# Row-block order for two w_out chunks of batch 0, paired P groups, and split output tiles in a one-core attention and MoE kernel

## Chip, cores, metric

One NeuronCore of a Trainium2 chip (trn2). The metric is device time in microseconds (us), the median of several runs of the whole kernel. A profile of one execution also gives a span, about 1.8 us shorter than the time of the same execution (215.9 and 217.67 for the kernel before); it is used for places and differences. In the lines of the profile, PE stands for TensorE's matmuls and PEld for its weight loads, DVE for VectorE, ACT for ScalarE, POOL for GpSimd and SP for SyncE; a q behind a name (SPq) marks the engine's queue of instructions. PSUM is the memory that matmuls write to. L476 is line 476 of that kernel's program.

## The reference

Eight batches, eight heads, 512 tokens and 32 state rows of width 64. Cross attention runs both ways between the tokens and the state; the result, 4352 rows of 512, goes through a feed-forward layer with exact Gelu.

```python
scores = scale * np.matmul(x, state.transpose(0, 1, 3, 2))
a = softmax(scores);  xread = np.matmul(a, state)
a2 = softmax(scale * np.matmul(state, x.transpose(0, 1, 3, 2)))
sread = np.matmul(a2, x)
attn = np.concatenate([xread, sread], axis=2)      # then to rows of H * D = 512
h = attn_rows @ w_in                               # 512 -> 2048
out = (0.5 * h * (1.0 + erf(h * inv_sqrt2))) @ w_out   # 2048 -> 512, float32
```

## The kernel before

The kernel folds w_in into the state: P = state @ w_in per batch, so that h = a @ P. A w_out chunk is four of the sixteen row blocks of h of a batch; a chunk of P is one P group, 512 of its 2048 columns. The order of instructions is written by hand. The pieces that matter:

```python
ps_f = ctx.enter_context(tc.tile_pool(name="ps_f", bufs=4, space=PSUM))   # hp, p_ps, transposes, sread
ps_o = ctx.enter_context(tc.tile_pool(name="ps_o", bufs=4, space=PSUM))   # output tiles, P chunks 3 and 4 of a run

def p_mm(b, f, pool, tag):            # a P group: 8 matmuls of 64x32 tiles, two PSUM buffers
    ps = [pool.tile([128, 512], FP32, name="p_ps", tag=tag) for t in range(2)]
    ...
def p_copy(b, f, ps):
    dst = Ps[b][:, :, f * 512:(f + 1) * 512]
    nc.scalar.copy(out=dst[:, 0, :], in_=ps[0])
    nc.vector.tensor_copy(out=dst[:, 1, :], in_=ps[1])

def mm1(b, m):                        # row block m of h, then Gelu on ScalarE
    hp = ps_f.tile([128, S], FP32, name="hp", tag="f")
    ...                               # two matmuls, P x AT
    nc.scalar.activation(out=gs[b][:, m, :], in_=hp, func=AF.Gelu)

def mm2(b, q, j):                     # output tile j: four row blocks of chunk q, one after the other
    ...
    for m in range(4 * q, 4 * q + 4):
        nc.tensor.matmul(ps, lhsT=gs[b][:, m, j * 128:(j + 1) * 128], rhs=w_out_bf[:, m, :],
                         start=(m == 0), stop=(m == MC - 1))
    if q == 3:
        evac(ps, [(out_rows(b, j), slice(0, 128))])   # VectorE copy, then a DMA from SyncE

# the order for batch 0 (cut); M = mm1 of these blocks, U = mm2
M(0, 1, 2, 3); U(0, 1, 2); pmat(0, 1); U(3)
...
M(10, 11); U(8); pmat(0, 3); U(9); atr(1); U(10); M(12, 13); srt(1); M(14, 15); U(11); pmat(1, 0)
...
U(12); state_prep(2, B); M(16); pmat(1, 1); U(13); M(17); U(14); M(18, 19); U(15)
burst([(1, 2), (1, 3), (2, 0), (2, 1)])
# steady pattern for batches 1 to 7 (cut)
mm2_sr(0); mm2_sr(1); U(*range(16 * B - 4, 16 * B - 1)); mm2_last(B - 1, SJ - 1)   # the last DMA leaves from ScalarE's queue
```

The softmax here doesn't subtract the row's maximum and nothing guards it: scores larger than these inputs give would overflow.

Of the kernel before, what the change touches and what calls it, by code (L numbers as in the profile page):

```python
# [9 lines left out]
FP32 = mybir.dt.float32  # L10
# [7 lines left out]
def kernel(  # L18
# [8 lines left out]
    nc = tc.nc  # L27

    B, H, S, D = x.shape
    _, _, NS, _ = state.shape  # L30
    d_model, d_ff = moe_w_in.shape
# [3 lines left out]
    MC = d_ff // 128  # L35
    SJ = S // 128
# [9 lines left out]
    ps_o = ctx.enter_context(tc.tile_pool(name="ps_o", bufs=4, space=PSUM))  # L46
# [6 lines left out]
    w_out_bf = persist.tile([128, MC, d_model], BF16, name="w_out_bf")  # L53
# [18 lines left out]
    for c in range(3):  # L72
# [5 lines left out]
        out=xbs[0].rearrange("p (t c) f -> p t c f", t=2)[:, :, 3, :], in_=x0_rows[:, :, 3, :]  # L78
# [56 lines left out]
    def state_prep(b0, b1):  # L135
        if b0 == 0:
            nc.scalar.copy(out=st_bf[:, 0, :, :], in_=st_f)
        n = b1 - b0
        ps = ps_f.tile([128, n, HC, NS], BF16, name="st_ps", tag="f")
        for b in range(b0, b1):  # L140
            nc.tensor.transpose(
                ps[:, b - b0, :, :].rearrange("p c n -> p (c n)"),
                st_bf[:, b, :, :].rearrange("q t d -> q (t d)"),
                ident,
            )
        for t in range(2):
            nc.vector.tensor_copy(
                out=sbd[64 * t:64 * t + 64, b0:b1, :, 32 * t:32 * t + 32].rearrange(
                    "d b c n -> d (b c) n"
                ),  # L150
                in_=ps[64 * t:64 * t + 64, :, :, :].rearrange("d b c n -> d (b c) n"),
            )
# [7 lines left out]
    def begin(b):  # L160
        A = Att()
        atts[b] = A
        A.x4 = x4s[b % 2]
        A.xo = xos[b % 2]
        A.xT = att.tile([128, SJ, HC, 128], BF16, name="xT", tag="xT")
        A.e = att.tile([128, SJ * 2, HC * NS], BF16, name="e", tag="e")
        A.a = att.tile([128, SJ * 2, HC * NS], BF16, name="a", tag="a")
# [133 lines left out]
    def atr(b):  # L301
        A = atts[b]
        A.AT = att.tile([128, SJ, 2, 128], BF16, name="AT", tag="AT")
        for t in range(2):
            ps = ps_f.tile([128, SJ, 128], BF16, name="aT_ps", tag="f")
            for j in range(SJ):
                nc.tensor.transpose(ps[:, j, :], A.a[:, 2 * j + t, :], ident)
            if b == 0 and t == 1:
                nc.scalar.copy(out=A.AT[:, :, t, :], in_=ps)
            else:  # L310
                nc.vector.tensor_copy(out=A.AT[:, :, t, :], in_=ps)
# [9 lines left out]
    def sread(b):  # L321
        A = atts[b]
        pool, tag = (ps_o, "op") if b == B - 1 else (ps_f, "f")
        A.sr = pool.tile([128, 2, 65], FP32, name="sr", tag=tag)
        for t in range(2):
            for j in range(SJ):
                for c in range(HC):
                    nc.tensor.matmul(  # L328
                        A.sr[32 * c:32 * c + 32, t, :],
                        lhsT=A.e[:, 2 * j + t, 32 * c:32 * c + 32],  # L330
                        rhs=A.xo[:, j, c, 1 + 65 * t:66 + 65 * t],
                        start=(j == 0),
                        stop=(j == SJ - 1),
                    )

    def sread_out(b):
        A = atts[b]
        A.srm = att.tile([128, 2, D], BF16, name="srm", tag="srm")
        flat = A.sr.rearrange("q t d -> q (t d)")
        inv = att.tile([128, 2], FP32, name="inv", tag="inv")  # L340
        nc.vector.reciprocal(out=inv, in_=flat[:, 0:130:129])
        nc.vector.tensor_tensor(
            out=A.srm,
            in0=flat[:, 1:129].rearrange("q (t d) -> q t d", t=2),
            in1=inv[:, :].to_broadcast((128, 2, D)),
            op=ALU.mult,
        )
# [11 lines left out]
    def p_mm(b, f, pool, tag):  # L359
        if b not in Ps:  # L360
            Ps[b] = att.tile([128, 2, d_ff], BF16, name="P", tag="P")
        ps = [pool.tile([128, 512], FP32, name="p_ps", tag=tag) for t in range(2)]
        for c in range(HC):
            for t in range(2):
                nc.tensor.matmul(  # L365
                    ps[t][32 * c:32 * c + 32, :],
                    lhsT=sbd[64 * t:64 * t + 64, b, c, 32 * t:32 * t + 32],
                    rhs=w_in_bf[64 * t:64 * t + 64, c, f * 512:(f + 1) * 512],
                    start=True,
                    stop=True,  # L370
                )
        return ps
# [6 lines that stand above are left out]
    def pmat(b, f):  # L379
        p_copy(b, f, p_mm(b, f, ps_f, "f"))  # L380
# [4 lines left out]
    def burst(chunks, b_read=None):  # L385
        done = []
        first = len(chunks) < 4 and b_read is not None
        if first:
            sread(b_read)
        for i, (b, f) in enumerate(chunks):  # L390
            pool, tag = (ps_f, "f") if i < 2 else (ps_o, "op")
            done.append((b, f, p_mm(b, f, pool, tag)))
        for x in done[:2]:
            p_copy(*x)
        if b_read is not None and not first:
            sread(b_read)
        for x in done[2:3]:
            p_copy(*x)
        if b_read is not None:
            sread_out(b_read)  # L400
        for x in done[3:]:
            p_copy(*x)
# [17 lines left out]
    gs = {}  # L420

    def mm1(b, m):
        if m == 0:
            gs[b] = gpool.tile([128, MC, S], BF16, name="g", tag="g")
        hp = ps_f.tile([128, S], FP32, name="hp", tag="f")
        for t in range(2):
            nc.tensor.matmul(  # L427
                hp,
                lhsT=Ps[b][:, t, m * 128:(m + 1) * 128],
                rhs=atts[b].AT[:, :, t, :],  # L430
                start=(t == 0),
                stop=(t == 1),
            )
        nc.scalar.activation(out=gs[b][:, m, :], in_=hp, func=AF.Gelu)  # L434

    ops = {}

    def evac(ps, rows):
        osb = opool.tile([128, d_model], FP32, name="osb", tag="osb")
        nc.vector.tensor_copy(out=osb, in_=ps)  # L440
        for r, src in rows:
            nc.sync.dma_start(out=r, in_=osb[src, :])

    def out_rows(b, j):
        return out[b * SB:b * SB + S, :].rearrange("(p j) n -> j p n", j=SJ)[j]
# [23 lines left out]
    def mm2(b, q, j):  # L469
        if b == B - 1 and j == SJ - 1:  # L470
            return
        if q == 0:
            ops[b, j] = ps_o.tile([128, d_model], FP32, name="op", tag="op")
        ps = ops[b, j]
        for m in range(4 * q, 4 * q + 4):
            nc.tensor.matmul(  # L476
                ps,
                lhsT=gs[b][:, m, j * 128:(j + 1) * 128],
                rhs=w_out_bf[:, m, :],
                start=(m == 0),  # L480
                stop=(m == MC - 1),
            )
        if q == 3:
            evac(ps, [(out_rows(b, j), slice(0, 128))])

    def mm1_sr(m):
        hp = ps_f.tile([128, B * NS], FP32, name="hps", tag="f")
# [10 lines left out]
    def mm2_sr(s):  # L498
        ps = ps_f.tile([128, d_model], FP32, name="ops", tag="f")
        for m in range(MC):  # L500
            nc.tensor.matmul(  # L501
                ps,
                lhsT=g_sr[:, m, s * 128:(s + 1) * 128],
                rhs=w_out_bf[:, m, :],
                start=(m == 0),
                stop=(m == MC - 1),
            )
        rows = []
        for i in range(4):
            r0 = (4 * s + i) * SB + S  # L510
            rows.append((out[r0:r0 + NS, :], slice(32 * i, 32 * i + 32)))
        evac(ps, rows)


    def M(*ms):
        for m in ms:
            mm1(m // MC, m % MC)

    def U(*us):
        for u in us:  # L520
            mm2(u // 16, u % 16 // 4, u % 4)
# [35 lines left out]


    M(0, 1, 2, 3)
    U(0, 1, 2)  # L560
    pmat(0, 1)
    U(3)
    M(4, 5)
    state_prep(1, 2)
    M(6)
# [17 lines left out]
    sread(1)  # L583
    sread_out(1)
    M(10, 11)
    U(8)
    pmat(0, 3)
    U(9)
    atr(1)
    U(10)  # L590
    M(12, 13)
    srt(1)
    M(14, 15)
    U(11)
    pmat(1, 0)
    begin(2)
    rearr(2)
    xtr_dma(2)
    rearr_ones(2)
    U(12)  # L600
    state_prep(2, B)
    M(16)
    pmat(1, 1)
    U(13)
    M(17)
    U(14)
    M(18, 19)
    U(15)
    burst([(1, 2), (1, 3), (2, 0), (2, 1)])


    u = 16
# [72 lines left out]
```

## Time and profile before

| | before |
|---|---|
| time, median (runs beside the changed kernel) | 217.70 us (217.56 to 217.81, 4 runs) |
| span of the profiled execution | 215.9 us |
| TensorE busy | 208.2 us, 96% |
| PE stretch | 197.60 us |
| last landing to end of span | 1.36 us |

The prediction had three of the four runs, with a median of 217.63.

### The profile page before, as it was taken

The numbers are of one execution on the slowest core, as the hardware profiler recorded it, in microseconds if no ns is written. First come the engines' busy times: TensorE is split into PE (matmuls) and PEld (weight loads), VectorE is DVE, ScalarE is ACT, GpSimd is POOL, SyncE is SP. The second block draws the span as 40 slices with busy tenths as digits, with TensorE's granted clock in tenths as the row PEclk, the third lists the DMA queues.
The fourth block names the chain that finished last, engine by engine and source line by source line (L and its number), as shares of the span: only waits on it lengthen the run. The fifth ranks groups of instructions, "written<-read, shape, count | busy, mean of one in ns | idle before, by whom it ended". The sixth has DMA issues, their size and how long they took to land.

```text
span 215.9 us, 3969 instructions
## 1 busy us (share of the span) xinstructions
PE 208.2 (96%) x1638; PEld 103.4 (48%) x1663; DVE 80.4 (37%) x165; ACT 122.7 (57%) x217; POOL 43.5 (20%) x57
## 2 busy tenths in 40 slices
PE   8889999999999999999999999999999999999993
PEld 8535444444444445444444444444444444765442
DVE  4815665724039202840177006900392025000151
ACT  3754846687686447844974477546864444754000
POOL 7583105901123013301321130300000000000000
PEclk9999999999999999999999999999999999999999
DMA  7999999972722591429350963170225013000044
GB/s 186 187 192 206 206 191 135 257 135 52 97 97 100 99 144 43 154 48 153 46 194 3 155 88 145 52 146 0 100 99 52 0 67 130 3 0 0 14 129 151
DMA packets 38723, 22.98 MB, mean 106 GB/s; under 512 B 21936, under 2 KB 34480, under 8 KB 38704
## 3 DMA queue, kind: packets, MB, share of 16 engines
q0 software_dynamic: 13664, 8.23, 27.1%
q1 hardware_dynamic: 24352, 14.09, 24.8%
q10 hardware_dynamic: 688, 0.39, 0.6%
q8 instruction: 13, 0.21, 0.4%
q14 instruction: 6, 0.05, 0.1%
HBM read 17.30 MB, written 8.91 MB: 121 GB/s over the span
## 4 chain that ended last, share of the span: by engine, by line
PE 93%; ACT 3%; DVE 1%; issue 1%
PE op L476 48%; PE hp L427 25%; PE p_ps L365 4%; PE hps L489 3%; PE ops L501 3%; PE warm_ps L132 2%; ACT g L434 2%; PE opl L454 2%; PE pt L271 2%; PE sr L328 1%; PE xT_ps L211 1%; ACT L434 1%; ACT P L376 1%; PE pc L230 0%; DVE xT L216 0%
## 5 line engine op out<-in xcount | busy, mean ns | idle before, releaser
L476 PE MATMUL op<-w_out_bf,g 128*128 128x512 bf16 x471 | 115.5, 379 | 1.7 <-ACT g L434 0.3
L434 ACT ACTIVATE g<-hp 128x512 bf16<-128x512 f32 x128 | 68.8, 602 | 55.3 <-PE hp L427 55.1
L476 PEld LDWEIGHTS <-g 128*128 128x128 bf16 x496 | 47.9, 98 | 58.3 <-ACT g L434 1.9
L427 PE MATMUL hp<-AT,P 128*128 128x512 bf16 x256 | 65.8, 379 | 0.8 <-ACT P L376 0.5
L440 DVE COPY osb<-op 128x512 f32<-128x512 f32 x31 | 21.4, 691 | 83.1 <-PE op L476 83.1
L427 PEld LDWEIGHTS <-P 128*128 128x128 bf16 x256 | 23.5, 98 | 27.4 <-issue 2.0
L377 DVE CAST P<-p_ps 128x512 bf16<-128x512 f32 x31 | 20.0, 683 | 9.4 <-PE p_ps L365 9.3
L376 ACT CAST P<-p_ps 128x512 bf16<-128x512 f32 x31 | 16.3, 595 | 12.0 <-PE p_ps L365 12.0
L175 POOL COPY x<-xb 128x1024 bf16<-128x1024 bf16 x12 | 12.2, 1043 | 31.5 <-DMA xb<-in_x_dram 26.5
L186 POOL COPY xo<-xb 128x1024 bf16<-128x1024 bf16 x12 | 12.2, 1048 | 22.3 <-PE sr L328 22.3
L291 DVE TENSOR_REDUCE cs<-e 128x16 f32<-128x512 bf16 x14 | 9.5, 677 | 3.9 <-ACT e L278 3.9
L365 PE MATMUL p_ps<-w_in_bf,sbd 64*32 64x512 bf16 x248 | 10.3, 382 | 0.0
L278 ACT ACT_TABLE_LOAD x7 | 9.0, 1283 | 2.1 <-issue 1.3
L294 DVE TENSOR_TENSOR a<-e,ics 128x512 bf16<-128x512 bf16 x14 | 9.7, 692 | 0.5
L440 DVE COPY osb<-ops 128x512 f32<-128x512 f32 x2 | 1.4, 692 | 22.5 <-PE ops L501 22.5
L434 ACT ACT_TABLE_LOAD x7 | 9.0, 1283 | 0.1
L465 ACT COPY osb<-opl 128x128 f32<-128x128 f32 x1 | 0.3, 266 | 15.2 <-PE opl L454 15.2
L278 ACT ACTIVATE e<-pt 128x512 bf16<-128x512 f32 x14 | 7.6, 594 | 0.1
L489 PE MATMUL hps<-XSR,w_in_bf 128*128 128x256 bf16 x64 | 7.6, 273 | 0.0
L132 PE MATMUL warm_ps<-warm 128*128 128x128 bf16 x59 | 6.5, 280 | 1.0 <-DVE warm L75 1.0
L501 PE MATMUL ops<-w_out_bf,g_sr 128*128 128x512 bf16 x32 | 7.1, 379 | 0.0
L365 PEld LDWEIGHTS <-sbd 64*32 64x32 bf16 x248 | 3.5, 89 | 7.5 <-issue 6.4
(66 smaller groups left out, 105.2 us busy)
## 6 DMA issues: line engine op xcount, KB each, us to landing
out_dram<-osb SPq DMA_DIRECT2D x31, 256.0 KB, 2.3
xb<-in_x_dram POOLq DMA_DIRECT2D x7, 512.0 KB, 6.0
w_in_bf<-in_moe_w_in_dram POOLq DMA_DIRECT2D x8, 256.0 KB, 9.6
w_out_bf<-in_moe_w_out_dram POOLq DMA_DIRECT2D x4, 512.0 KB, 11.5
x0f<-in_x_dram SPq DMA_DIRECT2D x2, 256.0 KB, 3.3
out_dram<-osb SPq DMA_DIRECT2D x8, 64.0 KB, 1.7
x0f<-in_x_dram ACTq DMA_DIRECT2D x1, 256.0 KB, 4.1
st_bf<-in_state_dram POOLq DMA_DIRECT2D x1, 192.0 KB, 14.3
```

What stands on the lines that cost most here:

```text
L175: nc.gpsimd.tensor_copy(out=A.x4[:, :, :, 64 * t:64 * t + 64].rearrange("p j c d -> p c j d"), in_=src[:, t],)
L186: eng.tensor_copy(out=A.xo[:, :, c0:, 2 + 64 * t:66 + 64 * t].rearrange("p j c d -> p c j d"), in_=src[:, t, c0:],)
L278: nc.scalar.activation(out=A.e[:, :, 64 * half:64 * half + 64], in_=pt.rearrange("p j t c n -> p (j t) (c n)"), func=AF.Exp, scale=scale,)
L365: nc.tensor.matmul(ps[t][32 * c:32 * c + 32, :], lhsT=sbd[64 * t:64 * t + 64, b, c, 32 * t:32 * t + 32], rhs=w_in_bf[64 * t:64 * t + 64, c ...
L376: nc.scalar.copy(out=dst[:, 0, :], in_=ps[0])
L377: nc.vector.tensor_copy(out=dst[:, 1, :], in_=ps[1])
L427: nc.tensor.matmul(hp, lhsT=Ps[b][:, t, m * 128:(m + 1) * 128], rhs=atts[b].AT[:, :, t, :], start=(t == 0), stop=(t == 1),)
L434: nc.scalar.activation(out=gs[b][:, m, :], in_=hp, func=AF.Gelu)
L440: nc.vector.tensor_copy(out=osb, in_=ps)
L476: nc.tensor.matmul(ps, lhsT=gs[b][:, m, j * 128:(j + 1) * 128], rhs=w_out_bf[:, m, :], start=(m == 0), stop=(m == MC - 1),)
L489: nc.tensor.matmul(hp, lhsT=w_in_bf[:, c, m * 128:(m + 1) * 128], rhs=XSR[:, c, :], start=(c == 0), stop=(c == HC - 1),)
L501: nc.tensor.matmul(ps, lhsT=g_sr[:, m, s * 128:(s + 1) * 128], rhs=w_out_bf[:, m, :], start=(m == 0), stop=(m == MC - 1),)
```

## The change

Its intent: the Gelu results of the first and third chunk come more slowly than TensorE uses them, so each ready row block is applied to all four output tiles before the next one is needed; P groups, each of which costs a change of the array's tiling, are gathered; and the last output tile of a batch leaves in two halves.

```diff
--- before.py
+++ after.py
@@ -438,8 +438,8 @@
     def evac(ps, rows):
         osb = opool.tile([128, d_model], FP32, name="osb", tag="osb")
         nc.vector.tensor_copy(out=osb, in_=ps)
-        for r, src in rows:
-            nc.sync.dma_start(out=r, in_=osb[src, :])
+        for r, src, n0, n1 in rows:
+            nc.sync.dma_start(out=r, in_=osb[src, n0:n1])
 
     def out_rows(b, j):
         return out[b * SB:b * SB + S, :].rearrange("(p j) n -> j p n", j=SJ)[j]
@@ -481,7 +481,9 @@
                 stop=(m == MC - 1),
             )
         if q == 3:
-            evac(ps, [(out_rows(b, j), slice(0, 128))])
+            rows = out_rows(b, j)
+            h = d_model // 2 if j == SJ - 1 else d_model
+            evac(ps, [(rows[:, n:n + h], slice(0, 128), n, n + h) for n in range(0, d_model, h)])
 
     def mm1_sr(m):
         hp = ps_f.tile([128, B * NS], FP32, name="hps", tag="f")
@@ -508,8 +510,21 @@
         rows = []
         for i in range(4):
             r0 = (4 * s + i) * SB + S
-            rows.append((out[r0:r0 + NS, :], slice(32 * i, 32 * i + 32)))
+            rows.append((out[r0:r0 + NS, :], slice(32 * i, 32 * i + 32), 0, d_model))
         evac(ps, rows)
+
+
+    def mm2_m(b, m):
+        for j in range(SJ):
+            if m == 0:
+                ops[b, j] = ps_o.tile([128, d_model], FP32, name="op", tag="op")
+            nc.tensor.matmul(
+                ops[b, j],
+                lhsT=gs[b][:, m, j * 128:(j + 1) * 128],
+                rhs=w_out_bf[:, m, :],
+                start=(m == 0),
+                stop=(m == MC - 1),
+            )
 
 
     def M(*ms):
@@ -557,9 +572,10 @@
 
 
     M(0, 1, 2, 3)
-    U(0, 1, 2)
+    for m in range(3):
+        mm2_m(0, m)
     pmat(0, 1)
-    U(3)
+    mm2_m(0, 3)
     M(4, 5)
     state_prep(1, 2)
     M(6)
@@ -583,30 +599,28 @@
     sread(1)
     sread_out(1)
     M(10, 11)
-    U(8)
-    pmat(0, 3)
-    U(9)
+    mm2_m(0, 8)
+    mm2_m(0, 9)
+    burst([(0, 3), (1, 0)])
+    mm2_m(0, 10)
     atr(1)
-    U(10)
     M(12, 13)
     srt(1)
     M(14, 15)
-    U(11)
-    pmat(1, 0)
+    mm2_m(0, 11)
     begin(2)
     rearr(2)
     xtr_dma(2)
     rearr_ones(2)
     U(12)
+    burst([(1, 1), (1, 2)])
+    U(13)
     state_prep(2, B)
-    M(16)
-    pmat(1, 1)
-    U(13)
-    M(17)
+    M(16, 17)
     U(14)
     M(18, 19)
     U(15)
-    burst([(1, 2), (1, 3), (2, 0), (2, 1)])
+    burst([(1, 3), (2, 0), (2, 1)])
 
 
     u = 16
```

## The prediction

> **What bounds the kernel now.** I read the page first, then the chain that ended last, then the waits of the matmul engine, then the instruction timelines of weight loads and ScalarE in the first 45 us, because the change edits nothing later except the last output tile of each batch.
>
> From the page, parts 1, 2 and 4:
>
> ```profile
> PE 208.2 (96%) x1638; PEld 103.4 (48%) x1663; DVE 80.4 (37%) x165; ACT 122.7 (57%) x217; POOL 43.5 (20%) x57
> PE   8889999999999999999999999999999999999993
> PEclk9999999999999999999999999999999999999999
> PE 93%; ACT 3%; DVE 1%; issue 1%
> ```
>
> TensorE is busy for 96% of a 215.9 us span at full granted clock, and 93% of the chain is PE. Only slices 1 to 3 and the last show holes. Each batch after the first runs the same pattern of matmuls back to back, so a reordering can gain only where PE waits. The list of PE's waits names little, but it sees only the matmul rows; a matmul that stands behind a late weight load appears under PEld. So the timeline of weight loads shows more. Columns: start us, length us, engine, line, operation, count, and in brackets the idle time and its releaser. First chunk of w_out, batch 0:
>
> ```profile
> 13.26 0.10 PEld L476 LDWEIGHTS <-g 128*128 128x128 bf16 x1
> 13.51 0.10 PEld L476 LDWEIGHTS <-g 128*128 128x128 bf16 x1 [0.16 <-ACT g L434]
> 14.00 0.10 PEld L476 LDWEIGHTS <-g 128*128 128x128 bf16 x1 [0.39 <-ACT g L434]
> 14.49 1.63 PEld L476 LDWEIGHTS <-g 128*128 128x128 bf16 x9 [0.40 <-ACT g L434]
> ```
>
> and the third chunk:
>
> ```profile
> 27.62 0.10 PEld L476 LDWEIGHTS <-g 128*128 128x128 bf16 x1
> 27.89 0.10 PEld L476 LDWEIGHTS <-g 128*128 128x128 bf16 x1 [0.17 <-ACT g L434]
> 28.38 0.10 PEld L476 LDWEIGHTS <-g 128*128 128x128 bf16 x1 [0.39 <-ACT g L434]
> 28.87 0.10 PEld L476 LDWEIGHTS <-g 128*128 128x128 bf16 x1 [0.40 <-ACT g L434]
> 29.19 0.11 PEld L365 LDWEIGHTS <-sbd 64*32 64x32 bf16 x8 [0.23 <-issue]
> ```
>
> In both, the first output tile walks through four row blocks of g, and each of blocks 1 to 3 is waited for. ScalarE supplies them thus:
>
> ```profile
> 12.38 2.07 ACT L434 ACTIVATE g<-hp 128x512 bf16<-128x512 f32 x4 [0.19 <-PE hp L427]
> 25.46 1.28 ACT L434 ACT_TABLE_LOAD   x1
> 26.75 2.07 ACT L434 ACTIVATE g<-hp 128x512 bf16<-128x512 f32 x4
> ```
>
> Four Gelus take 2.07 us, one about 0.60, so one block comes each 0.49 us, where PE can consume one each 0.216. These two places are what the change aims at.
>
> **What the Trainium skill says.** "TensorE: Matmul & The Clock Gate", Back-to-back issue gap: 512 columns warm cost 512/2.4 + 2.5 = 216 ns. The trace agrees: eight op matmuls take 1.73 us on the chain. Same page, The mechanism (part 3): weight loads may be pulled ahead, but matmuls keep strict program order. The trace agrees in that ready blocks of the other three tiles did not fill the holes above; hence the order in the program matters. "TensorEngine Tiling (Array Packing)", Key Properties: changing the tiling mode drains TensorE. The trace agrees: before a P group (64*32 tiles) the weight load starts 0.52 us after the previous one, not 0.216. "ScalarE: Activation LUTs", What ACT_TABLE_LOAD costs: 1283 ns plus a drain of about 1380. The load is the 1.28 us above; but Gelu starts right behind it (25.46 + 1.28 = 26.74), so no separate drain shows here, and the measurement stands.
>
> **The change part by part.**
>
> *First chunk.* Twelve weight loads start at 13.26, and the last at 14.49 + 1.63 - 0.10 = 16.02. Without waits the last starts at 13.26 + 11 x 0.216 = 15.63. Lost: 0.39 us. In the new order block 0 serves four tiles (0.86 us), then block 1, and so on: block 1 is wanted at 14.12 and is ready near 12.38 + 0.60 + 0.49 = 13.47; block 2 is wanted at 14.99 and ready near 13.96; block 3 comes after the P group. No wait remains: -0.39. The four output accumulators are wanted together a little earlier; their buffers were last read by the P copies, which end by 12.2.
>
> *Third chunk.* Four loads from 27.62 should end with the fourth at 28.27, and the P group's load should follow 0.52 later, at 28.79. It starts at 29.19. Lost: 0.40 us. In the new order block 8 is ready near 27.35 and wanted at 27.62, block 9 ready near 27.84 and wanted at 28.48; blocks 10 and 11 come later still. -0.40.
>
> *P in runs of two.* Cost of one P group between full-array matmuls, and of four in a run:
>
> ```profile
> 33.29 0.74 PEld L476 LDWEIGHTS <-g 128*128 128x128 bf16 x4
> 34.46 0.11 PEld L365 LDWEIGHTS <-sbd 64*32 64x32 bf16 x8 [0.42 <-issue]
> 34.80 0.55 PEld L476 LDWEIGHTS <-g 128*128 128x128 bf16 x4 [0.23 <-issue]
> ...
> 39.91 0.53 PEld L476 LDWEIGHTS <-g 128*128 128x128 bf16 x3
> 40.86 0.54 PEld L365 LDWEIGHTS <-sbd 64*32 64x32 bf16 x26 [0.42 <-issue]
> ...
> 42.05 0.98 PEld L427 LDWEIGHTS <-P 128*128 128x128 bf16 x6 [0.23 <-issue]
> ```
>
> Single: last load before it at 33.93, fourth after it at 35.25; 1.32 - 4 x 0.216 = 0.45 us. Run of four: 40.34 to 42.93 over six loads, 2.59 - 1.30 = 1.29. So a further chunk costs (1.29 - 0.45)/3 = 0.28, and each change of mode saved is worth 0.17. Before: five singles and one run of four, 5 x 0.45 + 1.29 = 3.54. After: singles (0,1) and (0,2), pairs (0,3)(1,0) and (1,1)(1,2), and a run of three, 0.90 + 2 x 0.73 + 1.01 = 3.37. -0.17.
>
> *What the shorter run loses.* The run of three is followed directly by the hp matmuls of block 20, which take the PSUM buffer of the run's first chunk, and that is free only when ScalarE has copied it. The last batch has the same case with a run of two:
>
> ```profile
> 179.15 0.14 PEld L365 LDWEIGHTS <-sbd 64*32 64x32 bf16 x16
> 179.63 1.07 ACT L376 CAST P<-p_ps 128x512 bf16<-128x512 f32 x2 [1.80 <-PE p_ps L365]
> 180.26 1.02 PE L427 MATMUL hp<-AT,P 128*128 128x512 bf16 x4 [0.48 <-ACT P L376]
> ```
>
> The buffer came free 1.11 us after the run's first load. A run of four lasts 42.05 - 40.86 = 1.19 and hides that; a run of three lasts 0.34 + 2 x 0.28 = 0.90. Stall: +0.21. The pairs are followed by four op matmuls (0.86 us, other buffers), so they are covered.
>
> *Output tile as two DMAs.* Seven more DMAs, each 128 KB in place of 256. They leave from SyncE, nothing on PE waits for them, and the output pool has four buffers. The transposes behind them in the queue have slack: the A transpose of batch 2 lands at 54.5 us by the trace's landing records and is first used at 56.5. 0.
>
> Sum: -0.39 - 0.40 - 0.17 + 0.21 = -0.75 us. All of it lies on PE's chain, and what follows is bound by PE, so it should reach the end: 217.63 - 0.75 = 216.88.
>
> **The rivals.** First, the loads: PE now reaches each weight and input 0.4 to 0.8 us earlier and could meet a transfer. Landing records: x of batch 1 at 17.56 (wanted 18.8), second w_out chunk 20.3 (wanted 21.3), third w_out chunk 26.2 (27.2), last w_in chunk 28.3 (29.2). About 1 us everywhere, so it should not bite, but load times vary; if one is late by 0.4 us more than its slack, the time is about 217.2.
>
> Second, ScalarE: from 21.2 to 28.8 it pauses only once, for 0.64 us before the copy of P at 24.86, which waits for PE. That wait says ScalarE follows PE, so its two table loads shift along. If it did not, the first 0.39 would be given back: near 217.3.
>
> Third, PSUM: the pair (0,3)(1,0) takes all four buffers of its pool at once, among them the sread result, which VectorE reads until 29.27 now and about 28.9 then; the pair's load falls at 29.26. Slack 0.4, with copies queued behind on VectorE. A miss would cost 0.1 to 0.3: about 217.1. Fourth, the other way, the stall after the run of three is smaller than I think, because ScalarE is less loaded: 216.7.
>
> **Range and chances.** The two removed waits (0.79) are read directly; the P terms nearly cancel and have the loosest signs. Adding 0.3 to 0.4 for a new wait of a rival gives the upper end, dropping the stall and 0.15 of small gaps gives the lower: 216.5 to 217.3. The whole disputed sum is under 0.5% of the time, so 2% is out of reach either way unless something unforeseen hits every batch.
>
> **What would show it.** In the changed profile: no PEld wait for g in the first and third chunks, with the first P group's load near 16.15 instead of 16.54; each pair costing 0.73 us; PE stopped for about 0.2 us behind the run of three, released by ScalarE's P copy; from there on the old pattern about 0.75 us earlier, with the same spacing per batch. Wrong it would be if PE newly waits for a DMA, or for VectorE before the pair, or if later batches change in length.

## More of the kernel before

The **PE stretch** runs from the first hp weight load of batch 0 (11.07 us in this trace) to the first weight load of the last output tile, by the instruction records of the trace.

The lines that carry the reading are in the prediction. Two more, left out there, turned out to matter. First the waits of the queues, SyncE's own, before (us in total, times, longest):

```profile
SPq L680 <- DMA out_dram<-osb: 1.9, 1, 1.9
```

and the end of the chain of waits, before (start us, length us, what):

```profile
209.05 3.51 PE opl L454 x32
212.56 0.02 issue
212.58 0.27 ACT osb L465
```

The work on engines ends at 212.85, but the span is 215.9. The 3.05 us between are one DMA and the ending of the program, and no view of the page lists the latter.

## The result, and the profile after

The changed kernel takes 216.32 us (216.11 to 216.51, 4 runs) against 217.70 us; the ratio is 0.9937, 95% interval 0.9919 to 0.9954. A ratio here is the mean time of one kernel's fast runs over that of the other's fast runs of the same rounds, so it is not quite the ratio of the quoted medians. The gain of 1.38 us was to be 0.75, and 216.32 lies below the range of 216.5 to 217.3. The whole change is under 1% of the time, so the intervals and the traces decide about the parts.

Page of the changed kernel, busy times and the chain's shares:

```profile
PE 208.8 (97%) x1663; PEld 103.6 (48%) x1663; DVE 79.8 (37%) x165; ACT 122.7 (57%) x217; POOL 43.6 (20%) x57
PE 96%; DVE 1%; ACT 1%; issue 0%
```

ScalarE's share of the chain falls from 3% to 1%. The busy PE time is no smaller; the before trace had 25 matmul records fewer, so these two cannot be subtracted. Timeline of weight loads, changed kernel, at the two chunks and at the run of three:

```profile
13.35 2.47 PEld L521 LDWEIGHTS <-g 128*128 128x128 bf16 x12
16.24 0.11 PEld L365 LDWEIGHTS <-sbd 64*32 64x32 bf16 x8 [0.42 <-issue]
...
27.32 1.61 PEld L521 LDWEIGHTS <-g 128*128 128x128 bf16 x8
29.35 0.14 PEld L365 LDWEIGHTS <-sbd 64*32 64x32 bf16 x16 [0.42 <-issue]
29.90 0.55 PEld L521 LDWEIGHTS <-g 128*128 128x128 bf16 x4 [0.42 <-issue]
...
38.97 0.74 PEld L476 LDWEIGHTS <-g 128*128 128x128 bf16 x4
40.14 0.35 PEld L365 LDWEIGHTS <-sbd 64*32 64x32 bf16 x24 [0.42 <-issue]
40.91 0.10 PEld L427 LDWEIGHTS <-P 128*128 128x128 bf16 x1 [0.42 <-issue]
41.25 1.39 PEld L427 LDWEIGHTS <-P 128*128 128x128 bf16 x7 [0.25 <-issue]
```

and the matmuls behind the run of three:

```profile
41.25 1.89 PE L427 MATMUL hp<-AT,P 128*128 128x512 bf16 x8 [0.27 <-ACT P L376]
```

The first chunk's twelve loads now stand in one row, 2.47 us long, with no wait for g; so do the eight of the third. The foreseen stall behind the run of three is there: hp starts 1.11 us after the run's first load (40.14 to 41.25), released by ScalarE's P copy. So far the prediction. But it is longer than foreseen: the first weight load for hp stands at 40.91, where the run of three is over, and its matmul starts at 41.25, so PE stands for 0.34 us, not 0.21. And the pairs are cheaper than foreseen. Around the first pair, the last load before it starts at 27.32 + 1.61 - 0.10 = 28.83 and the fourth after it at 29.90 + 0.55 - 0.10 = 30.35; 1.52 - 4 x 0.216 = 0.66 us, where the prediction said 0.73. The PE stretch is 196.70 us, 0.90 less than the 197.60 before.

The rest is at the end. The same two views as before:

```profile
SPq L694 <- DMA out_dram<-osb: 1.4, 2, 1.1
```

```profile
208.24 3.51 PE opl L454 x32
211.75 0.02 issue
211.78 0.27 ACT osb L465
```

From the last copy's start to the end of the span it was 215.90 - 212.58 = 3.32 us, and now 214.65 - 211.78 = 2.87. The last DMA itself takes the same: from issue to landing 1.66 us before and 1.65 after. From its landing to the end it is 1.36 and 0.93. SyncE's semaphore instructions, which the page doesn't count, tell why. Read from the records of the two traces (start in us; the record starts when the semaphores waited for are there; S107 and so on are semaphores):

```
before                              changed
212.65  wait S106, S105             211.84  wait S106, S105
214.56  wait S107, S104             211.91  wait S107, S104
214.62  wait S109, S103             211.98  wait S109, S103
214.68  wait S112, S102             212.04  wait S112, S102
214.74  wait S113, S101             212.10  wait S113, S101
214.80  wait S115, S100             212.16  wait S115, S100
214.86  wait S116, S99              212.22  wait S116, S99
214.92  wait S117, S108             213.38  wait S117, S108
214.98  wait S118, S114             213.74  wait S118, S114

last DMA lands: S107 at 214.54      last DMA lands: S118 at 213.72
```

The DMAs of the SyncE and ScalarE queues take eight semaphores in rotation: S107, S109, S112, S113, S115, S116, S117, S118 (the instruction of each DMA names its semaphore; there are 57 such DMAs before, 7 x 8 + 1, and 64 in the changed kernel). At the end SyncE waits for each, in that order, one in some 61 ns. Before, the last DMA of the program happened to hold the first of the list, so seven waits (0.43 us) came after it had landed. Seven halved tiles make seven DMAs more, which turns the rotation by seven of eight places. The last DMA now holds the last of the list, and the other waits are over before it lands. "Perfetto Trace Analysis", Sequencer-only Instruction, of the Trainium skill says that the profiler reports such an instruction from the moment its semaphores are satisfied, so the wait itself is not in its length; the trace agrees, since the record after the jump from 212.65 to 214.56 starts 0.02 us after the landing.

By the parts: 0.90 on the PE stretch and 0.43 at the end, 1.33 us together. The two spans differ by 1.25; the start took 0.09 us longer in the changed kernel's trace, which makes up the difference. This account was a reading of two traces, so it was tried.

### The profile page after: what moved, and what is told of

Read it like the earlier page. It is cut to its first block, busy times and chain, and to the rows that moved or that the text cites. A ratio compares the mean times of both kernels' runs of the same rounds, so it can differ in the third digit from the quotient of the medians.

```text
span 214.7 us, 4002 instructions
## 1 busy us (share of the span) xinstructions
PE 208.8 (97%) x1663; PEld 103.6 (48%) x1663; DVE 79.8 (37%) x165; ACT 122.7 (57%) x217; POOL 43.6 (20%) x57
## 4 chain that ended last, share of the span: by engine, by line
PE 96%; DVE 1%; ACT 1%; issue 0%
PE op L476 47%; PE hp L427 26%; PE p_ps L365 4%; PE op L521 3%; PE hps L491 3%; PE ops L503 3%; PE warm_ps L132 2%; PE opl L454 2%; PE pt L271 2%; PE sr L328 1%; PE xT_ps L211 1%; ACT P L376 1%; PE pc L230 0%; DVE xT L216 0%; PE xT_ps L208 0%; PE aT_ps L307 0%
## 5 line engine op out<-in xcount | busy, mean ns | idle before, releaser
L476 PE MATMUL op<-w_out_bf,g 128*128 128x512 bf16 x464 | 110.0, 379 | 0.0
L476 PEld LDWEIGHTS <-g 128*128 128x128 bf16 x464 | 45.2, 98 | 53.8 <-issue 0.6
L521 PE MATMUL op<-w_out_bf,g 128*128 128x512 bf16 x32 | 7.7, 380 | 0.0
```

Of the source, the lines that this page charges most:

```text
L521: nc.tensor.matmul(ops[b, j], lhsT=gs[b][:, m, j * 128:(j + 1) * 128], rhs=w_out_bf[:, m, :], start=(m == 0), stop=(m == MC - 1),)
```

## The experiments

Twelve more runs were made, one of them of the changed kernel again, all with correct results. Kernels are compared only within the same rounds.

| run | time, median | before, same rounds | ratio (95%) | PE stretch | landing to end |
|---|---|---|---|---|---|
| changed | 216.32 | 217.70 | 0.9937 (0.9919 to 0.9954) | 196.70 | 0.93 |
| split_only | 217.04 | 217.54 | 0.9977 (0.9965 to 0.9989) | 197.63 | 0.91 |
| after_nosplit | 216.67 | 217.54 | 0.9957 (0.9945 to 0.9969) | 196.85 | 1.35 |
| split_eight | 217.69 | 217.54 | 1.0008 (0.9994 to 1.0023) | 197.61 | 1.36 |
| one_moved | 217.20 | 217.54 | 0.9981 (0.9969 to 0.9992) | 197.61 | 0.90 |
| first_only | 217.14 | 217.72 | 0.9986 (0.9972 to 1.0000) | 197.22 | 1.36 |
| third_only | 217.27 | 217.72 | 0.9981 (0.9969 to 0.9993) | 197.20 | 1.34 |
| p_only | 217.42 | 217.72 | 0.9988 (0.9976 to 1.0000) | 197.49 | 1.35 |
| cover_three | 216.35 | 217.72 | 0.9950 (0.9934 to 0.9966) | 196.54 | 0.91 |
| after_again | 216.34 | 217.73 | 0.9936 (0.9924 to 0.9948) | 196.70 | 0.91 |
| cover_swap | 216.26 | 217.73 | 0.9935 (0.9921 to 0.9950) | 196.54 | 0.92 |
| split_four | 217.25 | 217.73 | 0.9980 (0.9967 to 0.9992) | 197.61 | 1.11 |
| evac_twice | 218.79 | 217.73 | 1.0048 (1.0029 to 1.0066) | 198.33 | 1.34 |

Run times of one kernel spread over 0.2 to 1.3 us, so for single parts the last two columns are the sharper measure, and the ratios say whether the time goes along. For first_only and p_only the interval reaches 1.0000: their times alone do not show a gain; the stretch does.

### The split alone, and the change without it

split_only is the kernel before with just this (and the matching change of `evac`, cut here; it is that of the whole change):

```diff
-            evac(ps, [(out_rows(b, j), slice(0, 128))])
+            rows = out_rows(b, j)
+            h = d_model // 2 if j == SJ - 1 else d_model
+            evac(ps, [(rows[:, n:n + h], slice(0, 128), n, n + h) for n in range(0, d_model, h)])
```

> The kernel before with nothing but the last output tile of batches 0 to 6 sent as two DMAs. Theory W (the end of the program): SyncE at the end waits for eight DMA semaphores in a fixed order, some 61 ns each; the DMAs of the hardware queues take these eight in rotation, and the very last DMA of the kernel before holds the first of the list, so that seven waits remain to be walked after it has landed. Seven more DMAs turn the rotation by seven, the last DMA gets the last place, and the walk is over before it lands: 0.43 us less (217.3 us), with the PE stream unchanged. Rival S (the prediction): the split does nothing, 217.7. Rival Q: smaller DMAs clear the queue sooner; then the gain would show as earlier landings, not behind the last landing.

after_nosplit is the changed kernel with `h = d_model` in that place.

> The changed kernel with whole output tiles again. Theory W: the last DMA holds the first place of the list again, 0.43 us more than the changed kernel, so about 216.75, that is 0.95 us less than before, all of it on PE. Rival S: as the changed kernel, 216.3. From the last landing to the end of the span: 1.33 us under W (as before), 0.90 under S.

Measured: the split alone takes 0.50 us off the median and 0.45 off what follows the landing (1.36 to 0.91); the PE stretch is that of before. Taking the split out of the changed kernel brings 1.35 us back behind the last landing, and the time is 216.67 us. Rival S, which was the prediction's own step, is wrong.

after_nosplit has a PE stretch 0.15 us longer than the changed kernel's, though nothing but later DMAs differs. Its timeline of weight loads shows where:

```profile
29.02 0.28 PEld L365 LDWEIGHTS <-sbd 64*32 64x32 bf16 x16 [0.42 <-issue]
```

The pair's sixteen loads are spread over 0.28 us instead of 0.14. By the landing records the last piece of w_in, which this pair reads, landed at 29.12 in this execution (28.10 in the changed kernel's), and the pair's second load starts at 29.16. So the prediction's first rival, a load that is late, does occur in some executions, at a cost of 0.15 us.

### Is it the rotation, or the smaller DMAs?

Three kernels, all with the PE order of before. split_eight (here against split_only) splits one tile more, so that the rotation comes round once:

```diff
-            h = d_model // 2 if j == SJ - 1 else d_model
+            h = d_model // 2 if j == SJ - 1 or (b == 0 and j == SJ - 2) else d_model
```

> The kernel before with eight output tiles sent as two DMAs (the last of batches 0 to 6, and one more of batch 0). Theory W: eight more DMAs turn the rotation of eight semaphores once round, the last DMA holds the first place again, and the gain is gone: 217.7, as before. Rival Q (smaller DMAs clear the queue sooner): at least the gain of seven splits, 217.3.

one_moved splits nothing, but takes one small DMA out of the rotation:

```diff
-        for r, src in rows:
-            nc.sync.dma_start(out=r, in_=osb[src, :])
+        for i, (r, src) in enumerate(rows):
+            eng = nc.gpsimd if moved and i == 0 else nc.sync      # moved: first tile of the state rows only
+            eng.dma_start(out=r, in_=osb[src, :])
```

> The kernel before with no tile split, but one of the eight small DMAs of the state rows' output issued from GpSimd's queue, which has semaphores of its own. Theory W: one DMA fewer in the rotation is the same as seven more, the last DMA gets the last place of the list: 217.3. Rival Q and Rival S: nothing is split, 217.7.

split_four (against split_only) stops half way:

```diff
-            h = d_model // 2 if j == SJ - 1 else d_model
+            h = d_model // 2 if j == SJ - 1 and b < 4 else d_model
```

> The kernel before with only the last output tiles of batches 0 to 3 as two DMAs: four DMAs more. Theory W: the last DMA holds the fifth of eight places, three waits of 61 ns remain behind it, so 1.36 - 4 x 0.061 = 1.11 us from the last landing to the end, and 0.24 us less than before (217.4). Rival Q (smaller DMAs clear the queue): the last three batches and the end are as before, so 1.36 and 217.65.

Measured: with eight splits the last DMA holds S107 again, 1.36 us follow its landing, and the gain is gone (ratio 1.0008). With no split and one DMA fewer, it holds S118, 0.90 us follow, and the ratio is 0.9981. With four splits it holds S115, and 1.11 us follow, as worked out beforehand. The gain goes with the place in the list, not with the size or number of the DMAs. The issue-to-landing time of the last DMA lies between 1.65 and 1.68 us in all these traces, so rival Q is out. For split_four the ratio alone (0.9980) would not tell a gain of 0.24 us from one of 0.43; the trace does.

### The two chunks, each alone

first_only (the definition of `mm2_m`, as in the whole change, is cut in both):

```diff
-    U(0, 1, 2)
+    for m in range(3):
+        mm2_m(0, m)
     pmat(0, 1)
-    U(3)
+    mm2_m(0, 3)
```

> The kernel before with only the first w_out chunk of batch 0 by row blocks. By the prediction's step: 0.39 us less, 217.3, the twelve weight loads of the chunk 0.216 us apart without a wait for g, all later PE work 0.39 us earlier. Rival A (ScalarE or a load gives it back): the first P group is 0.39 earlier, but by 30 us PE is as late as before, 217.7.

third_only:

```diff
-    U(8)
+    mm2_m(0, 8)
+    mm2_m(0, 9)
     pmat(0, 3)
-    U(9)
+    mm2_m(0, 10)
     atr(1)
-    U(10)
     ...
-    U(11)
+    mm2_m(0, 11)
```

> The kernel before with only the third w_out chunk of batch 0 by row blocks, P groups single as before. By the prediction's step: 0.40 us less, 217.3; the P group's weight load follows the chunk's eight loads with no wait for g. Rival A: a wait for the P copies or for w_in takes its place, 217.5 to 217.7.

Measured on the PE stretch: 0.38 and 0.40 us less, as the prediction had them (0.39 and 0.40), and all of it arrives at the end of the stretch. Rival A finds nothing. The times agree with that (0.9986 and 0.9981; 0.9982 was to be expected), though the interval of first_only also reaches 1.

### The P groups alone

```diff
-    U(8); pmat(0, 3); U(9); atr(1); U(10)          # shortened
+    U(8, 9); burst([(0, 3), (1, 0)]); U(10); atr(1)
-    pmat(1, 0); ... U(12); state_prep(2, B); M(16); pmat(1, 1); U(13); M(17)
+    ... U(12); burst([(1, 1), (1, 2)]); U(13); state_prep(2, B); M(16, 17)
-    burst([(1, 2), (1, 3), (2, 0), (2, 1)])
+    burst([(1, 3), (2, 0), (2, 1)])
```

> The kernel before with only the P groups in runs of two and three. The prediction's step: 0.17 us less for the change of mode, 0.21 more for the stall behind the run of three, so 0.04 more, 217.7. Theory V (after the result): a second chunk in a run costs 0.21 us, not 0.28, because the 0.28 was an average over a run of four whose last chunk waits for VectorE to clear the last output tile's PSUM buffer; then each pair costs 0.66 and the whole is 0.12 less than before, 217.6. The spacing of weight loads decides: 0.66 (V) or 0.73 (prediction) per pair, and no gap inside pairs and inside the run of three.

The PE stretch is 0.11 us shorter, near theory V's 0.12 and not 0.04 longer. The three parts alone give 0.38 + 0.40 + 0.11 = 0.89 us, and together they gave 0.90: they add up.

Why the prediction's 0.28 per further chunk was too much shows in the run of four of the kernel before, in the line that the prediction's fence left out. Weight loads before, with the line ahead of it:

```profile
40.86 0.54 PEld L365 LDWEIGHTS <-sbd 64*32 64x32 bf16 x26 [0.42 <-issue]
41.72 0.10 PEld L365 LDWEIGHTS <-sbd 64*32 64x32 bf16 x6 [0.31 <-issue]
```

and VectorE at that time, before:

```profile
40.97 0.69 DVE L440 COPY osb<-op 128x512 f32<-128x512 f32 x1 [1.03 <-PE op L476]
```

The run stops for 0.31 us after 26 of its 32 loads, and goes on 0.06 us after VectorE has finished copying the last output tile of batch 0 (40.97 + 0.69 = 41.66). One of the fourth chunk's two PSUM buffers is that of this tile. evac_twice was made to test it: the copy is made twice, which changes no data.

```diff
-        nc.vector.tensor_copy(out=osb, in_=ps)
+        for _ in range(2 if twice else 1):          # twice: b == 0 and j == 3 only
+            nc.vector.tensor_copy(out=osb, in_=ps)
```

> The kernel before with VectorE's copy of the output tile before the run of four made twice (same data, same result). Theory V: the fourth chunk of that run waits for this copy; the gap before its last six weight loads grows from 0.31 to about 0.9 us, the first 26 loads stay as they are, and PE is about 0.6 us later behind the run (218.2), perhaps a little more for the P copies queued behind. Rival (the gap is the run's own pace): the gap stays 0.31; PE is late only where hp waits for VectorE's P copies, by up to 0.5.

Weight loads and matmuls of evac_twice:

```profile
41.44 0.54 PEld L365 LDWEIGHTS <-sbd 64*32 64x32 bf16 x26 [0.42 <-issue]
43.02 0.10 PEld L365 LDWEIGHTS <-sbd 64*32 64x32 bf16 x6 [1.04 <-issue]
```

```profile
43.02 0.41 PE L365 MATMUL p_ps<-w_in_bf,sbd 64*32 64x512 bf16 x7 [0.54 <-DVE osb L441]
```

The gap grows from 0.31 to 1.04 us, at the same place, and the PE stretch by 0.73 us, one VectorE copy. Now the matmul row names VectorE as well; in the kernel before the short wait was put down to "issue". So a chunk in a run costs about 0.21 us (0.66 - 0.45 from the pair), and the run of four had 0.2 us of waiting in it that I took for its pace.

The time of evac_twice grew by more than the stretch, 1.05 us by the ratio, where 0.6 was expected. In the profiled execution the stretch also began 0.58 us later, because a piece of w_in that the start waits for landed at 10.76 and not at 9.29; that is not the copy's doing. The other runs of it have no profile.

The same break, 26 loads and then 0.31 or 0.32 us, stands in four of the five later runs of four of the kernel before (it ends at 65.53, 111.43, 134.32 and 157.22 us, each time 0.05 or 0.06 us after a VectorE copy of an output tile), and the change leaves those runs as they are. By the 0.2 us of the first run each may cost about as much; this is an estimate, and no run tried to remove them.

### The stall behind the run of three, and a version meant to beat both

cover_three is the changed kernel with the last output tile of batch 0 put around the run of three:

```diff
-    U(15)
-    burst([(1, 3), (2, 0), (2, 1)])
+    mm2_ms(0, 3, (12, 13))        # two of the tile's four matmuls
+    burst([(1, 3), (2, 0), (2, 1)])
+    mm2_ms(0, 3, (14, 15))        # the other two, then the copy and its two DMAs
```

> The changed kernel with two of the four matmuls of the output tile before the run of three put behind it. If the 0.2 us stall behind the run of three is the wait for ScalarE's first P copy, two matmuls into another PSUM buffer (0.43 us) hide it: 0.2 us less than the changed kernel, about 216.1. If something else holds PE there (mode change, P of batch 1 not ready), no gain: 216.3.

The PE stretch falls by 0.17 us, to 196.54, so the stall can be filled with other work, as it should be if hp waits for ScalarE's first P copy (the releaser that the changed kernel's trace names). The gain is half of the 0.34 us, and the weight loads of cover_three show why:

```profile
39.73 0.12 PEld L365 LDWEIGHTS <-sbd 64*32 64x32 bf16 x10 [0.42 <-issue]
40.11 0.14 PEld L365 LDWEIGHTS <-sbd 64*32 64x32 bf16 x14 [0.27 <-issue]
```

The run now starts two matmuls earlier and breaks for 0.27 us after ten loads. By the records the run's tenth matmul waits for a semaphore of ScalarE and starts at 40.11, after the Gelu of block 19 has ended at 40.06. From the run's first load to the next full-array load it is 0.93 us, and 0.77 in the changed kernel, so 0.16 us of the gain is lost there.

The time of 216.35 us shows no gain; two of its six runs took 217.04 and 217.20, the other four from 216.13 to 216.41. This lot had no run of the changed kernel on the same chip, so the next lot has one (after_again), next to cover_swap, which also turns the pair round so that the late piece of w_in is read second:

```diff
-    burst([(0, 3), (1, 0)])
+    burst([(1, 0), (0, 3)])
```

> The changed kernel itself once more, as the partner on one chip for the next kernel: 1.2 to 1.4 us less than before; PE from the first hp weight load to the first of the last tile 196.70 us, as in the first trace of it.

> A version meant to beat both: the changed kernel with the stall behind the run of three covered (two matmuls of the last output tile behind it; 0.17 us off the PE stretch in the run that tried it) and with the pair turned round, batch 1 first, so that the last piece of w_in, which once came 0.1 us late, has 0.2 us more. PE stretch 196.53, time 0.15 to 0.3 us less than the changed kernel of the same rounds; if the swap makes a copy late for the transposes or for block 12, the stretch is longer than 196.60.

after_again repeats the changed kernel in stretch (196.70), end (0.91) and time. cover_swap keeps the shorter stretch (196.54), but its ratio of 0.9935 cannot be told from 0.9936. Its own runs go from 215.98 to 216.96. So the expected 0.15 to 0.3 us is there on PE and not shown in the time. The swap shows nothing of its own: in none of these two profiles was w_in late.

## Why the prediction was wrong, step by step

- **First chunk, 0.39 us, and third chunk, 0.40 us: right.** Alone they measured 0.38 and 0.40.
- **P groups, 0.17 less for the changes of mode: mis-sized.** The term was the further chunk's 0.28 us, an average over a run of four. The pair measured 0.66 instead of 0.73, a further chunk 0.21, and so a saved change of mode 0.24 instead of 0.17; the rest of the average was a wait for VectorE, which evac_twice lengthened at will. The line with the gap was in the answer that I quoted from, and my fence skipped it with an ellipsis.
- **Stall behind the run of three, 0.21 more: right in mechanism, mis-sized by the same term.** hp started 1.11 us after the run's first load, as read from the last batch. But with the cheaper chunks the run itself is over after 0.77 us, not 0.90, so the stall was 0.34. The two errors partly cancel: the P part came to 0.11 us less where the prediction had 0.04 more.
- **"Output tile as two DMAs ... 0": wrong, and the largest error.** It measured 0.43 to 0.45 us less. The working asked whether anything on PE waits for these DMAs, and found nothing, rightly. It did not ask what follows PE: 1.36 us from the last landing to the end, 0.43 of them seven semaphore waits that stood behind the last DMA only because of where the rotation had come to.
- **"All of it lies on PE's chain": true of the three other parts only.** Sum as it was: 0.38 + 0.40 + 0.11 + 0.43 = 1.32 us, against 1.38 between the medians and 0.9937 x 217.70, that is 1.37 less, by the ratio.
- **The rivals.** The late load occurred, in one trace, for 0.15 us instead of 0.4. ScalarE moved along with PE (its Gelus of the third chunk at 26.45, before 26.75). The PSUM wait before the pair did not occur, and the stall was larger, not smaller. The direction that cost the range was upwards in speed, for which only the 0.21 of the stall and 0.15 us of small gaps had been allowed.

Still open: whether the 0.16 us of cover_three reach the time; that needs many more runs, since the start alone varies by more. What makes the start vary was not looked into, except for the late piece of w_in in evac_twice.

## What to carry to other kernels

Ask of every added or removed DMA also what it does to the ending: here which semaphore the last transfer gets decides whether a walk over seven others, 0.43 us, is hidden or not, and one DMA more or fewer changes it, so a small change of time after any edit of DMA counts may be nothing else. Before an average over a run of instructions is used as a price, look for a gap inside the run. And where row blocks come from a slower engine, use each for all tiles before the next: that was worth just what the gaps between weight loads said.

## What the Trainium skill lacked or had wrong

- Ending of a program: no page names the one-by-one waits for DMA semaphores, or that the rotation decides how many stand behind the last landing. "Runtime: NRT & Kernel Launch", The ~15µs preamble/postamble breakdown, has about 1.5 us for a barrier at the end and no such waits. The traces here have 0.90 to 1.36 us from the last landing to the end of the span, 61 ns for each wait left; no run here shows whether that is the same barrier.
- "TensorE: Matmul & The Clock Gate", Back-to-back issue gap: it gives about 131 ns for a 512-column matmul in a real stream of weight loads and matmuls. The traces show 216 ns (eight in 1.73 us) all through the stretch; its formula for the isolated gap, which the prediction used, is the one that holds here.
- "TensorEngine Tiling (Array Packing)", Key Properties: it says that a change of tiling mode drains the array, with no figure. Here a single group of eight 64x32 matmuls between full-array ones costs 0.45 us, and a second group in the same run 0.21 more, which leaves, as an estimate, 0.24 us for the two changes of mode.
- "ScalarE: Activation LUTs", What ACT_TABLE_LOAD costs: the load is 1.28 us as the page says; the drain of about 1.38 us that it adds does not show on either side of this kernel's table load, which starts at 25.46, behind a copy that ends at 25.45, and is followed by a Gelu at 26.75.
